# Moving the upper side of SBUF down by 224 bytes, and 128 free bytes between two pools

## The chip, the cores and the metric

The kernel runs on one core of a Trainium2 chip. The core's engines work side by side, each through its own list of instructions: TensorE (PE in the profile; its weight loads stand apart as PEld), VectorE (DVE), ScalarE (ACT), GpSimd (POOL), and SyncE (SP), which here only issues DMAs. [...] The metric is the time of one execution on the device in microseconds, the median of several runs.

A matmul has two operands in SBUF. The **stationary** one (`lhsT`, 128 by 128 here) is loaded into the array by a weight load, LDWEIGHTS in the profile. The **moving** one (`rhs`, 128 by 512) is streamed past it.

## The reference, cut to what matters

```
attention, separately in each chunk of 64 positions (8 batches, 8 heads, 576 positions, 64 wide):
    scores = q_c @ k_c^T / 8;  attn = softmax(scores);  out = attn @ v_c
x = out as (4608 tokens, 512)
h = x @ w_in                          # 512 -> 2048
g = h * clip(h + 3, 0, 6) / 6
result = g @ w_out                    # 2048 -> 512
```

All inputs and outputs are float32.

## The kernel before

**Blocks and stages.** The 4608 tokens are cut into nine blocks of 512. The first three (`NSTD = 3`) are computed in the plain way: `mm1` makes one of the 16 slices `ft` of `h`, `mm2` adds its share to the four output tiles. `SEGMENTS` gives the order: block 0 with slices 0 to 3, block 1 with slices 0 to 15, block 0 with slices 4 to 15, block 2 with slices 0 to 15. The other six blocks go in three pairs through Strassen's scheme with seven products in place of eight (`first_product`, `second_product`, lines 507 to 619). Attention of later blocks is woven between the products of earlier ones.

**Every product in three passes.** A float32 number is split into a rounded part and the rest, so `passes` (lines 220 to 224) issues three matmuls with 512 moving columns each: high by high, high by low, low by high.

```
222        PE.matmul(ps, lhsT=a_h, rhs=b_h, start=first, stop=False, skip_group_check=more)
223        PE.matmul(ps, lhsT=a_h, rhs=b_l, start=False, stop=False, skip_group_check=more)
224        PE.matmul(ps, lhsT=a_l, rhs=b_h, start=False, stop=last, skip_group_check=more)
```

In the plain stage the stationary operand is a part of a weight tile `w0` to `w15`, and the moving one is `x` (in `mm1`) or `g` (in `mm2`). Each slice of a block takes 12 matmuls in `mm1` and 12 in `mm2`, so the plain stage has 3 x 16 x 24 = 1152 of them. In the stage of the pairs the stationary operand is a part of a streamed weight tile `ws`, and the moving one is an operand tile `xop`; there are 3 x (8 x 7 x 2 x 3 + 7 x 8 x 2 x 3) = 2016 of them.

**Where tiles lie in SBUF.** Pools are stacked from two ends: most grow upwards from the bottom (the lower side), those with `side="right"` downwards from the top (the upper side). [...] The addresses that decide what follows, as the built program lists them:

| tile | role in the matmul | first byte | remainder by 64 |
|---|---|---|---|
| `w0` ... `w7` (upper side, line 57) | stationary, plain stage | 163,808 + 8192 k | 32 |
| `w8` ... `w15` (lower side, line 59) | stationary, plain stage | 39,104 + 8192 (k - 8) | 0 |
| `x` of blocks 0 to 2 (lower side) | moving, `mm1` | 22,720; 30,912; 104,640; 112,832 | 0 |
| `g` (lower side) | moving, `mm2` | 121,024 + 4096 k | 0 |
| `xop` (upper side, line 465) | moving, pairs | 163,808 + 8192 k | 32 |
| `ws` (upper side, line 466) | stationary, pairs | 139,232; 147,424; 155,616 | 32 |

The parts of a tile that a matmul reads start at multiples of 512 bytes within it. So the distance from the moving to the stationary operand has one of two remainders by 512: 0 (`w8` to `w15` with `x` or `g`, and `ws` with `xop`) or 288, which is 32 by 256 and by 64 (`w0` to `w7` with `x` or `g`).

**Change of pools.** At slot `FREE` (lines 460 to 469) the pools of the plain stage's upper side are closed: `sums` (tiles `a`, `hl`, `o`), `start` (`part`), `upper` (`w0` to `w7`). The pools `xop` (eight tiles) and `wsp` (three tiles) are opened in their place, and the first three weight tiles are fetched by SP. A tile waits for the last use of whatever lay at its bytes. From slot `SUMS` on (line 454) each engine's order is the one in which the program's lines are written; before it, a scheduler orders them.

**The start.** POOL clears `r` (line 65, called `nought` in the code), then makes `ident` (line 67). 11 matmuls on `nought` and later 56 on `ident` (line 81) keep TensorE busy while the first loads are on their way; their results are not used.

## Time and profile before

| what | value |
|---|---|
| time, median of 3 runs (lowest, highest) | 825.01 us (824.76, 825.08) |
| span of the profiled execution, first to last instruction | 822.7 us |
| mean granted TensorE clock | 1.000 |
| matmuls in the profile, all kinds | 5683 |

The profile was taken in an execution of its own, whose time the page gives as its span; 2.3 us lie between that and the median of the runs.

How to read it: a line of a group gives the source line, the engine, the operation, the tiles written and read, the shapes and the count; then the busy time in microseconds and the mean duration of one in nanoseconds, and the idle time of the engine ahead of it with what ended it. Matmuls are pipelined and their ends are modelled, so their durations overlap and say little of the pace; the pace is the distance between two starts. The view of stages gives, for each stretch, the busy time of each engine with the number of instructions that fall in it (also in part).

### The profile page before, as it was taken

To read this page: it belongs to the slowest core of one execution; us is meant where nothing else is said; L and a number is where in the kernel's file an instruction comes from. 1 tells how busy PE (TensorE), PEld (TensorE's weight loads), DVE (VectorE), ACT (ScalarE), POOL (GpSimd) and SP (SyncE) were. 2 spreads that over 40 slices of the span, in tenths; PEclk is the share of its full clock that TensorE was granted. 3 is DMA by queue.
4 is the path that set the end of the run, shared out by engine and by line. 5 is a ranking of instruction groups with operands and counts; after the bars stand their busy time and mean duration, and the time that the engine had idled before them with its cause. 6 is when DMAs were issued, how large, how long until landed. Compare 5 with 4: busy or idle time off the path is not lost.

```text
span 822.7 us, 13679 instructions
## 1 busy us (share of the span) xinstructions
PE 802.9 (98%) x5683; PEld 650.3 (79%) x5683; DVE 620.4 (75%) x753; ACT 367.1 (45%) x455; POOL 131.7 (16%) x77
## 2 busy tenths in 40 slices
PE   7889999999999999999999999999999999999998
PEld 5667888888878888788788887888788887878886
DVE  5869977877786864876989667778898567679951
ACT  4858934443444343434373432344634423336330
POOL 0000000000010000122272031222440312227100
PEclk9999999999999999999999999999999999999999
DMA  9892026677685761665646677566555664555563
GB/s 366 325 371 117 1 70 220 206 254 244 189 296 173 256 257 51 226 216 204 239 180 218 242 244 255 177 223 255 185 199 189 231 220 179 183 207 187 190 230 129
DMA packets 50158, 172.86 MB, mean 210 GB/s; under 512 B 4656, under 2 KB 17200, under 8 KB 39344
## 3 DMA queue, kind: packets, MB, share of 16 engines
q1 hardware_dynamic: 49952, 171.85, 59.3%
q8 instruction: 45, 0.74, 0.4%
q14 instruction: 17, 0.14, 0.1%
q10 hardware_dynamic: 144, 0.13, 0.0%
HBM read 133.17 MB, written 38.80 MB: 209 GB/s over the span
## 4 chain that ended last, share of the span: by engine, by line
PE 77%; DVE 13%; ACT 5%; issue 3%; DMA 1%; POOL 0%; SPq 0%; DVEq 0%; ACTq 0%
PE acc L222 17%; PE acc L224 16%; PE acc L223 16%; PE h L222 8%; PE h L224 8%; PE h L223 8%; DVE xop L381 2%; PE two L195 2%; DMA w<-w_in_out 1%; PE two L184 1%; DVE g L505 1%; DVE u L493 1%; PE two L155 1%; DVE e L165 1%; ACT r L504 1%
## 5 line engine op out<-in xcount | busy, mean ns | idle before, releaser
L222 PE MATMUL acc<-xop,ws 128*128 128x512 f32 x528 | 208.5, 396 | 4.4 <-DVE u L493 4.4
L223 PE MATMUL acc<-xop,ws 128*128 128x512 f32 x528 | 205.7, 390 | 0.0
L224 PE MATMUL acc<-xop,ws 128*128 128x512 f32 x528 | 205.3, 390 | 0.0
L222 PEld LDWEIGHTS acc<-xop,ws 128*128 128x128 f32 x528 | 99.1, 188 | 27.6 <-DVE u L493 6.8
L381 DVE TENSOR_TENSOR xop<-g,xop 128x1024 fp32r<-128x1024 f32 x72 | 103.3, 1467 | 21.5 <-ACT xop L380 21.5
L224 PEld LDWEIGHTS acc<-xop,ws 128*128 128x128 f32 x528 | 99.1, 188 | 21.1
L223 PEld LDWEIGHTS acc<-xop,ws 128*128 128x128 f32 x528 | 99.2, 188 | 19.7
L380 ACT CAST xop<-g 128x1024 fp32r<-128x1024 f32 x72 | 74.4, 1051 | 78.8 <-PE acc L224 51.3
L513 POOL TENSOR_TENSOR g<-g 128x512 f32<-128x512 f32 x24 | 34.8, 1449 | 301.2 <-DVE g L505 301.2
L222 PE MATMUL h<-x,w 128*128 128x512 f32 x192 | 76.1, 398 | 2.0 <-ACT x L204 0.9
L222 PE MATMUL acc<-g,w 128*128 128x512 f32 x192 | 76.6, 401 | 1.2 <-ACT g L236 1.2
L223 PE MATMUL h<-x,w 128*128 128x512 f32 x192 | 75.7, 394 | 0.5 <-DVE x L207 0.5
L224 PE MATMUL h<-x,w 128*128 128x512 f32 x192 | 75.5, 393 | 0.3 <-DVE w L117 0.3
L224 PE MATMUL acc<-g,w 128*128 128x512 f32 x192 | 75.4, 393 | 0.0
L223 PE MATMUL acc<-g,w 128*128 128x512 f32 x192 | 75.3, 392 | 0.0
L235 DVE SCALAR_TENSOR_TENSOR r<-r,h 128x512 f32<-128x512 f32 x48 | 32.8, 683 | 36.8 <-ACT r L234 36.7
L504 ACT ACTIVATE r<-acc,half 128x512 f32<-128x512 f32 x72 | 48.6, 687 | 26.2 <-DVE acc L493 25.3
L504 ACT ACTIVATE r<-h,half 128x512 f32<-128x512 f32 x24 | 16.5, 688 | 94.4 <-DVE h L493 94.4
L223 PE MATMUL h<-xop,ws 128*128 128x512 f32 x144 | 56.2, 390 | 0.1
L222 PE MATMUL h<-xop,ws 128*128 128x512 f32 x144 | 56.3, 391 | 0.0
L224 PE MATMUL h<-xop,ws 128*128 128x512 f32 x144 | 56.1, 389 | 0.0
L234 ACT ACTIVATE r<-h,half 128x512 f32<-128x512 f32 x48 | 33.0, 688 | 47.3 <-PE h L224 47.1
(92 smaller groups left out, 1255.3 us busy)
## 6 DMA issues: line engine op xcount, KB each, us to landing
ws<-b SPq DMA_DIRECT2D x42, 1024.0 KB, 4.9
ws<-a SPq DMA_DIRECT2D x24, 1024.0 KB, 4.9
ws<-a SPq DMA_DIRECT2D x24, 768.0 KB, 4.2
qk<-qk_in SPq DMA_DIRECT2D x17, 1024.0 KB, 6.5
w<-w_in_out SPq DMA_DIRECT2D x16, 1024.0 KB, 13.3
v<-v_in SPq DMA_DIRECT2D x17, 512.0 KB, 5.2
a<-hl SPq DMA_DIRECT2D x32, 256.0 KB, 3.3
b<-hl SPq DMA_DIRECT2D x32, 256.0 KB, 3.1
```

The costliest lines, as they stand in the source:

```text
L155: PE.matmul(self.s[o, a, c, :], lhsT=self.qk[rows, 0, c, o], rhs=self.qk[rows, 1, c, o], start=True, stop=True)
L165: DVE.tensor_tensor(out=flat(self.e), in0=flat(self.s), in1=wide(self.m), op=ALU.subtract)
L195: PE.matmul(po[o, s, a, i, :], lhsT=self.v[rows, a, i, o], rhs=self.aT[rows, a, i, o], start=True, stop=True)
L222: PE.matmul(ps, lhsT=a_h, rhs=b_h, start=first, stop=False, skip_group_check=more)
L223: PE.matmul(ps, lhsT=a_h, rhs=b_l, start=False, stop=False, skip_group_check=more)
L224: PE.matmul(ps, lhsT=a_l, rhs=b_h, start=False, stop=last, skip_group_check=more)
L234: ACT.activation(out=r, in_=h, func=AF.Relu, bias=half, scale=1.0 / 6.0)
L235: DVE.scalar_tensor_tensor(out=r, in0=r, scalar=1.0, in1=h, op0=ALU.min, op1=ALU.mult)
L380: ACT.copy(out=t[:, :, 0], in_=src)
L381: DVE.tensor_tensor(out=t[:, :, 1], in0=src, in1=t[:, :, 0].bitcast(F32), op=ALU.subtract)
L504: return (lambda: ACT.activation(out=r, in_=ps, func=AF.Relu, bias=half, scale=1.0 / 6.0), lambda: DVE.scalar_tensor_tensor(out=out, in0=r ...
L513: sub = lambda o, x, y: lambda: POOL.tensor_tensor(out=o, in0=x, in1=y, op=ALU.subtract)
```

## The change

A tile of 224 bytes is put on the upper side ahead of every other, and a tile of 128 bytes between the pools `xop` and `wsp`. Each is cleared once by POOL, and neither is read.

```diff
@@ -36,6 +36,8 @@
 WARM = 11
 WARM2 = (0, 36, 0, 6, 4)
 LAG = 2
+EDGE = 224
+GAP = 128
@@ -54,6 +56,8 @@
     std = ExitStack()
     upper = ExitStack()
+    edge = pool("edge", 1, side="right").tile([P, EDGE // 4], F32, name="edge")
+    POOL.memset(edge, 0.0)
     w_up = upper.enter_context(tc.tile_pool(name="w_up", bufs=1, side="right"))
@@ -463,6 +467,8 @@
                     upper.close()
                     xop_pool = pool("xop", 8, side="right")
+                    gap = pool("gap", 1, side="right").tile([P, GAP // 4], F32, name="gap")
+                    POOL.memset(gap, 0.0)
                     wsp = pool("wsp", 3, side="right")
                     for _ in range(3):
                         fetch()
```

So `w0` to `w7` and `xop` start at 163,584 + 8192 k (remainder 0 by 256), and `ws` at 138,880, 147,072 and 155,264 (remainder 128 by 256). Tiles of the lower side stay where they are (remainder 192 by 256). The distance from the moving to the stationary operand becomes 64 by 512 for `w0` to `w7` with `x` or `g`, 384 by 512 (128 by 256) for `ws` with `xop`, and stays 0 for `w8` to `w15`.

## The prediction

> **What bounds the kernel now.** First the page: its head, the busy times, the slices, the chain.

> ```profile
> span 822.7 us, 13679 instructions
> PE 802.9 (98%) x5683; PEld 650.3 (79%) x5683; DVE 620.4 (75%) x753; ACT 367.1 (45%) x455; POOL 131.7 (16%) x77
> PE   7889999999999999999999999999999999999998
> PEclk9999999999999999999999999999999999999999
> PE 77%; DVE 13%; ACT 5%; issue 3%; DMA 1%; POOL 0%; SPq 0%; DVEq 0%; ACTq 0%
> ```

> TensorE is busy 98% of the span at its full granted clock, and 77% of the chain that ended last is its own. What it does there is almost all matmuls of 512 columns. Such a kernel gets faster by fewer matmuls, fewer waits, or a quicker **pace**, the distance between two starts. The change touches neither the first nor, by its code, the second. So I read the pace, by the view in order of time, in three stretches without a wait: with `w1` to `w7` as stationary operands (plain stage, weights on the upper side, `x` and `g` on the lower), with `w8` to `w12` (both on the lower side), and in the pairs (`ws` and `xop`, both on the upper side). First and last start of each, then the view of stages, which counts:

> ```profile
> 73.74 0.40 PE L224 MATMUL h<-x,w 128*128 128x512 f32 x1
> ...
> 98.94 0.40 PE L224 MATMUL acc<-g,w 128*128 128x512 f32 x1
> 110.69 0.40 PE L224 MATMUL acc<-g,w 128*128 128x512 f32 x1
> ...
> 122.94 0.39 PE L224 MATMUL h<-x,w 128*128 128x512 f32 x1
> 424.73 0.39 PE L222 MATMUL acc<-xop,ws 128*128 128x512 f32 x1
> ...
> 444.91 0.39 PE L224 MATMUL h<-xop,ws 128*128 128x512 f32 x1
> ```

> ```profile
> 74.00:99.00 25.00, 25.00 (x109) 20.14 (x108) 24.62 (x31) 24.71 (x30) 0.00 (x0) 1.00 0.00 1
> 111.00:123.00 12.00, 12.00 (x55) 9.93 (x54) 8.89 (x16) 3.57 (x5) 0.00 (x0) 1.00 0.35 111
> 425.00:445.00 20.00, 20.00 (x90) 16.57 (x89) 20.00 (x11) 8.71 (x10) 11.55 (x4) 1.00 0.52 188
> ```

> The columns are the stretch, its length, and the busy time and count of PE, PEld, DVE, ACT and POOL, then clock and DMA. 109 matmuls are 108 distances: 25.20 us / 108 = 233.3 ns. The second gives 12.25 / 54 = 226.9 ns, the third 20.18 / 89 = 226.7 ns. The same instruction at the same clock takes 6.6 ns (2.9%) longer where the stationary operand lies 32 bytes off the moving one (288 by 512) than where it lies 0 off. The second stretch rules out "plain stage" as the reason, and the third, where both operands have remainder 32 by 64, rules out the remainder alone: **the distance counts**. The stretches' DMA shares (0.00, 0.35, 0.52) go the other way. This is the only thing in the trace on which a shift of addresses can act at length.

> **The change part by part.**

> *The plain stage.* Distance 32 by 256 becomes 64 by 256 for `w0` to `w7`. No row shows 64. The nearest are 32 (233.3 ns) and 0 (226.7 ns). Since both operands with remainder 0 by 64 run as quickly as both with 32, I take a repeat of 64 bytes: 64 acts as 0, and each matmul wins 6.6 ns. The other end is that 64 costs twice what 32 does: 6.6 ns lost. How many count: 3 blocks x 8 slices x 24 = 576. What precedes 66 us waits for loads and conversions; that is block 0's four slices and two `mm1` of block 1, 96 + 24 = 120. The chain also leaves TensorE for about 22 us:

> ```profile
> 215.93 0.24 PE h L224
> ...
> 234.64 1.29 issue
> 235.93 1.76 DVE g L237
> 237.68 0.61 DVE o L263
> 238.34 0.50 PE acc L222
> ```

> There the order written for DVE ends last, so what TensorE wins between 216 and 238 us (two `mm1`, 24 matmuls) only lengthens its wait. What it won ahead of 216 us is kept, since the chain comes from TensorE there. Left are 432 x 6.6 ns = 2.85 us. DVE may take some of it back: in the first stretch above it was busy 24.62 of 25.00 us and ACT 24.71, so its slack of 1.5% covers only half of the 2.9% that the 108 distances there (0.7 us) would win. I strike 0.4 us: **-2.4 us**. Ends: +2.85 us, and -6.0 us by the floor below.

> *The stage of the pairs.* Distance 0 becomes 128 by 256 for 2016 matmuls: the big lever. By a repeat of 64 bytes 128 is 0 again, and the term is **0**. No row shows 128, so both ends stay open. Worse: the 32-byte price, 2016 x 6.6 = +13.3 us. Better is bounded by the quickest pace per column in the trace, the warm-up's two-byte matmuls of 256 columns:

> ```profile
> 10.56 4.00 PE L81 MATMUL h<-ident 128*128 128x256 bf16 x35
> L81 PE MATMUL h<-ident 128*128 128x256 bf16 x56 | 6.6, 273 | 0.0
> ```

> (4.00 - 0.27) / 34 = 109.7 ns, twice that is 219.4 ns for 512 columns, 7.3 ns under the 226.7: -14.7 us for the pairs, and (233.3 - 219.4) x 432 = -6.0 us for the plain stage. The trace thus shows room below the quicker pace, but nothing that says that 128 bytes open it. I take the value of the nearest row, 0.

> [...]

> *The clearing of `edge`* goes to POOL ahead of `r`, for which the first warm-up matmul waits.

> ```profile
> L65 POOL MEMSET r<- 128x512 f32 x1 | 0.5, 525 | 0.3 <-POOLq L670 0.3
> masks.py:197 POOL MEMSET ident<- 128x128 f32 x1 | 0.2, 205 | 0.0
> L670 POOL MEMSET const-float32-0.0<- 128x1 f32 x1 | 0.1, 99 | 0.2 <-issue 0.2
> 2.80 11.63 DMA w<-w_in_out
> 14.45 1.13 ACT u L108
> ```

> Between 1 column (99 ns) and 128 (205 ns) its 56 columns take about 0.15 us. Queued behind it on POOL are `r` and `ident`; the warm-up waits for them, and is hidden by the load of `w0`, which carries the chain to 14.4 us. Cost 0; uncovered 0.15 us. Ahead of slot `SUMS` a scheduler orders the engines; one more instruction could make it pick another order. I see no reason for one, and put up to 0.5 us either way on it.

> *The clearing of `gap`* (32 columns, about 0.13 us) stands on POOL between these two:

> ```profile
> 234.43 2.71 POOL L261 TENSOR_TENSOR o<-o,part 128x512 f32<-128x512 f32 x2 [232.66 <-ACT o L260]
> 335.77 1.29 POOL L513 TENSOR_TENSOR g<-g 128x512 f32<-128x512 f32 x1 [98.63 <-DVE g L505]
> 287.55 1.84 SPq L359 DMA_DIRECT2D b<-hl  x4
> 293.82 1.28 SPq L375 DMA_DIRECT2D ws<-a  x3
> ```

> Its bytes last held `part`, read for the last time by L261 and L263 at 237 us. POOL idles for 98 us there, nobody waits for `gap`, and SP's queue is not touched. Cost 0. The 352 bytes by which `ws` sinks make its three tiles reach 128 bytes further down than the sum of their old covers: the first onto one more `o` tile (sent long before), the second onto `a`, the third onto `hl`. The stores of `hl` at 287.55 us were already waited for by the second fetch, ahead of the third on SP. So no new wait ends late, and `ws` has until 324 us.

> *Other engines.* Durations on DVE, ACT and POOL and the landing of `ws` (4.9 us, three tiles ahead) I cost at 0: TensorE's backlog hides them.

> Sum: -2.4 + 0 + 0 + 0 against the profiled 822.7 us, so a span of about 820.3; the runs' median lies 2.3 us above the span, so 825.0 - 2.4 = **822.6 us**.

> **The rivals.**

> *The pairs get quicker.* Were the reads of both operands to collide by 128 bytes and not by 64, a distance of 128 could be better than 0. For it: 226.7 ns is not the floor. Against: no row has it. With the 32-byte step again (6.6 ns) -13.3 us on the pairs and -2.4: 809.3 us; at the floor 825.0 - 14.7 - 6.0 = 804.3 us.

> *The pairs get slower.* The mechanism that costs 32 bytes 6.6 ns reaches `ws` with `xop`, as soon as its repeat is longer than 128 bytes and the best distance is 0. For it: 0 is the best distance that the trace shows. Against: both known distances fit a repeat of 64. Price 13.3 - 2.4: 835.9 us. It decides from 1.2 ns a matmul on, since 2016 x 1.2 = 2.4 us.

> *Only the plain stage gets slower.* The price grows with the distance (repeat 128): 64 costs 13.2 ns. 825.0 + 2.85 = 827.9 us.

> [...]

> **How the numbers follow.** Forecast 0.42 (its own range 821.6 to 823.6), pairs quicker 0.22, pairs slower 0.12, plain stage slower 0.10, nothing 0.14. A measurement of this kernel tells 0.2% (1.65 us) from no change. Faster: 0.22 and nearly all of the forecast's, 0.39, so 0.61; same: 0.14 and 0.03, so 0.17; slower: 0.22. A range from 803 (floor in both stages) to 829 leaves out the slower pairs and some tails, 0.18.

> **What the profile would show.** Right: in the stretch with `w1` to `w7` a pace of 226.7 ns in place of 233.3, the pairs still at 226.7, the wait at 238 us a little longer. Wrong: any other pace in the pairs, from 1.2 ns on; the plain stage at 233 or 240 ns; a PE wait for DVE between 74 and 100 us that eats the gain; another order of the instructions ahead of slot `SUMS`; a fetch of `ws` that starts well after 294 us.

## The result and the profile after

The changed kernel takes 833.38 us (median of four runs; 833.26 to 834.28) against 825.05 us before (four runs too): a ratio of 1.010, 95% interval 1.0088 to 1.0113. It is slower by 8.3 us where 2.4 us less were forecast, and it lies above the forecast range, which ended at 829 us.

The page of the changed kernel: span and busy times.

```profile
span 831.4 us, 13682 instructions
PE 813.7 (98%) x5683; PEld 651.2 (78%) x5683; DVE 620.7 (75%) x753; ACT 367.5 (44%) x455; POOL 132.0 (16%) x79
```

TensorE is busy 10.8 us longer with the same 5683 matmuls at the same granted clock (1.000 in both profiles); the other engines' busy times move by 0.4 us at most. The loss sits in the matmuls themselves. To see where, take the first and last starts of the matmuls of the pairs, by the view of the tile `ws` (minimum, median and maximum duration in ns, then first and last start in us). The kernel before comes first, then the changed one, where the same source lines have numbers higher by four:

```profile
L222 PE MATMUL acc<-xop,ws x528: 387/389/506, 324.6 to 807.3; 128*128 128x512 f32 x176
L224 PE MATMUL h<-xop,ws x144: 388/389/397, 327.8 to 818.6; 128*128 128x512 f32 x144
```

```profile
L226 PE MATMUL acc<-xop,ws x528: 390/393/504, 324.7 to 815.6; 128*128 128x512 f32 x176
L228 PE MATMUL h<-xop,ws x144: 390/393/404, 327.9 to 827.3; 128*128 128x512 f32 x144
```

The pairs begin at 324.6 and 324.7 us, so the plain stage neither won nor lost. From there to the last matmul it is 494.0 us before and 502.6 us after: the 8.6 us of the pairs are all but 0.1 us of the 8.7 by which the spans differ. The pace in the changed kernel, read as in the prediction, by first and last start and by the count in the view of stages:

```profile
73.81 0.39 PE L226 MATMUL h<-x,w 128*128 128x512 f32 x1
...
98.77 0.40 PE L228 MATMUL acc<-g,w 128*128 128x512 f32 x1
424.79 0.39 PE L228 MATMUL acc<-xop,ws 128*128 128x512 f32 x1
...
445.00 0.40 PE L228 MATMUL h<-xop,ws 128*128 128x512 f32 x1
```

```profile
74.00:99.00 25.00, 25.00 (x108) 20.12 (x107) 24.56 (x31) 24.68 (x30) 0.00 (x0) 1.00 0.00 1
425.00:445.00 20.00, 20.00 (x88) 16.20 (x87) 20.00 (x10) 8.43 (x9) 12.30 (x4) 1.00 0.48 168
```

Plain stage with `w1` to `w7`: 24.96 us / 107 = 233.3 ns, as before, though the distance from the moving to the stationary operand went from 32 to 64 bytes (by 256). Pairs: 20.21 / 87 = 232.3 ns in place of 226.7, at distance 128.

Now take every distance between two successive starts of the pairs' matmuls in the two traces. Those of up to 260 ns (about 1950 in both) sum to 442.9 us before and 454.2 us after, +11.4 us. The longer ones, at breaks for attention's matmuls and waits, sum to 51.1 and 48.4 us, -2.7 us. So a quarter of what the pace cost came back. Most of it is a wait of TensorE for DVE that got shorter:

```profile
PE acc L222 <- DVE u L493: 4.4, 6, 1.2
```

```profile
PE acc L226 <- DVE u L499: 2.6, 4, 0.7
```

Those are lines of the view of waits of the kernel before and of the changed one (us in total, times, longest): 1.8 us of the 2.7. The other 0.9 us were not traced to a wait.

The two clearings and the first fetch, by the changed kernel's view in order of time:

```profile
0.73 0.14 POOL L60 MEMSET edge<- 128x56 f32 x1 [0.29 <-POOLq L676]
238.96 0.13 POOL L471 MEMSET gap<- 128x32 f32 x1 [1.87 <-DVE o L267]
293.64 1.28 SPq L379 DMA_DIRECT2D ws<-a  x3
```

They take 0.14 and 0.13 us, `r` starts 0.08 us later than before (0.81 in place of 0.73 us), and the fetch starts no later (293.82 us before). None of it is the cause.

The new tile at the top did change the scheduler's order a little, which the forecast had named as a sign of being wrong. In the kernel before, DVE makes `g` (line 173) at 19.32 us and a `u` (line 109) two instructions later; in the changed kernel `u` comes first, at 19.42 us, and `g` at 20.02. The eight transposes on TensorE that need this `g` start at 21.39 in place of 20.70 us, and ten matmuls of attention's scores now stand ahead of them. It costs next to nothing: at 66 us TensorE stands 0.16 us ahead of the kernel before, where `gap_only`, which has the old order, stands 0.19 us behind it. `edge_only` below has the new order too.

### The profile page after: what moved, and what is told of

It reads as the page before. It is cut to its first block, busy times and chain, and to the rows that moved or that the text cites. A ratio compares the mean times of both kernels' runs of the same rounds, so it can differ in the third digit from the quotient of the medians.

```text
span 831.4 us, 13682 instructions
## 1 busy us (share of the span) xinstructions
PE 813.7 (98%) x5683; PEld 651.2 (78%) x5683; DVE 620.7 (75%) x753; ACT 367.5 (44%) x455; POOL 132.0 (16%) x79
## 2 busy tenths in 40 slices
PE   7889999999999999999999999999999999999998
## 4 chain that ended last, share of the span: by engine, by line
PE 84%; DVE 10%; ACT 4%; issue 1%; POOL 0%; DVEq 0%; ACTq 0%; POOLq 0%
PE acc L226 18%; PE acc L228 17%; PE acc L227 17%; PE h L226 9%; PE h L228 8%; PE h L227 8%; PE two L199 2%; PE two L188 1%; PE two L159 1%; DVE u L499 1%; DVE m L166 1%; DVE e L169 1%; ACT r L510 1%; DVE z L173 1%; ACT e L170 1%
## 5 line engine op out<-in xcount | busy, mean ns | idle before, releaser
L226 PE MATMUL acc<-xop,ws 128*128 128x512 f32 x528 | 211.2, 401 | 2.8 <-DVE u L499 2.6
L227 PE MATMUL acc<-xop,ws 128*128 128x512 f32 x528 | 208.4, 395 | 0.0
L228 PE MATMUL acc<-xop,ws 128*128 128x512 f32 x528 | 207.9, 395 | 0.0
L226 PE MATMUL h<-xop,ws 128*128 128x512 f32 x144 | 57.0, 396 | 0.0
L228 PE MATMUL h<-xop,ws 128*128 128x512 f32 x144 | 56.9, 395 | 0.0
L227 PE MATMUL h<-xop,ws 128*128 128x512 f32 x144 | 56.8, 394 | 0.0
```

## Experiments

One theory and its rivals to begin with. **D**: the pace is set by the distance, and all is lost in the pairs. The **rivals**: the place of the upper side itself (A), another order ahead of slot `SUMS` (O), a wait or the clearing at the new tile (W). All edits are made to the kernel before.

### The two parts alone

`edge_only` has the first part of the diff alone, `gap_only` the second:

```diff
+    edge = pool("edge", 1, side="right").tile([P, 224 // 4], F32, name="edge"); POOL.memset(edge, 0.0)
```

> The 224 bytes at the top alone; ws and xop sink together, so their distance stays 0, and w0 to w7 stand 64 bytes off x and g. Theory D (the pace is set by the distance from the moving to the stationary operand, and the loss sits in the pairs): pairs at 226.7 ns, plain stage with w1 to w7 at 233.4 ns as in the changed kernel, 825.0 us within 0.6. Rival A (the upper side's own place, remainder 0 by 256, is what costs): pairs near 232 ns and 833 us. Rival O (another order ahead of slot SUMS, or the clearing of edge): the pairs at 226.7 ns, yet 2 us or more lost ahead of 324 us.

```diff
+                    gap = pool("gap", 1, side="right").tile([P, 128 // 4], F32, name="gap"); POOL.memset(gap, 0.0)
```

> The 128 bytes between the pools alone; ws stands 128 bytes off xop, w0 to w7 stay 32 by 256 off x and g. Theory D: the whole loss is here, pairs near 232 ns, plain stage at 233.3 ns, 833.4 us within 0.8. Rival A: pairs at 226.7 ns and 825 us, since xop keeps its old place. Rival W (a late first fetch of ws): the pairs' first matmul later than 324.6 us by more than 1 us, and the pace in the pairs 226.7 ns.

The 224 bytes alone: 824.85 us, ratio 1.000 (0.9991 to 1.0009). The 128 bytes alone: 833.16 us, ratio 1.010 (1.0086 to 1.0114), and the pairs' first and last starts, by the view of `ws` of `gap_only`:

```profile
L222 PE MATMUL acc<-xop,ws x528: 390/393/504, 324.8 to 815.5; 128*128 128x512 f32 x176
L224 PE MATMUL h<-xop,ws x144: 390/393/404, 328.1 to 827.1; 128*128 128x512 f32 x144
```

That is 502.3 us for the pairs, as in the changed kernel. The gap carries the whole loss. A falls, since `xop` and `w0` to `w7` with remainder 0 by 256 cost nothing in `edge_only` (824.85 us); O falls with it, since that kernel has the clearing of `edge` and the other order too. W as a late first fetch falls as well, since the pairs begin at 324.8 us. That the new tile itself costs something is still open.

### The same tile with 256 bytes

```diff
+                    gap = pool("gap", 1, side="right").tile([P, 256 // 4], F32, name="gap"); POOL.memset(gap, 0.0)
```

> As the 128 bytes alone, with 256 bytes in their place: the same tile, clearing on POOL and covers of the old tiles, only the distance of ws from xop is a multiple of 256. Theory D with a repeat of 256 bytes: 226.7 ns in the pairs and 825.0 us within 0.6. Rival W (what costs is the tile between the pools, its clearing or the waits of the ws tiles on other old tiles): 833 us as with 128 bytes.

824.87 us, ratio 1.0002 (0.9992 to 1.0011). The same tile at the same place, cleared and waited for in the same way, costs nothing when it is 256 bytes wide; the pairs take 493.9 us, as in the kernel before (494.0). W falls altogether; the distance by 256 decides.

### Distances 0 and 256 in the plain stage

`edge_288` and `edge_32` have 288 and 32 bytes in place of the 224, and no gap.

> 288 bytes at the top and no gap: w0 to w7 stand a multiple of 512 off x and g, ws and xop stay at 0. Theory D: the plain stage with w1 to w7 at 226.7 ns, the pairs unchanged, 2.4 us gained (1.9 to 2.9), so 822.6 us, faster than both kernels. Rival A: no gain, 825 us. Rival V (what the plain stage wins is lost to DVE, which was 98% busy between 74 and 99 us): pace 226.7 ns, but new waits and under 1 us gained.

> 32 bytes at the top and no gap: w0 to w7 stand 256 by 512 off x and g. Theory D with a repeat of 256 bytes: as with 288 bytes, 226.7 ns and 822.6 us. Theory D with a repeat of 512 bytes or more: the plain stage still near 233 ns, 825.0 us within 0.5. The upper side has remainder 192 by 256 then, like the lower side; under a theory of equal remainders by 256 it is quick too.

288 bytes: 822.81 us, ratio 0.9975 (0.9965 to 0.9984). 32 bytes: 822.67 us, ratio 0.9976 (0.9967 to 0.9985). Both are faster than both kernels, by about the gain that the forecast had ascribed to 64 bytes, so rival V, with under 1 us gained, falls. `edge_288` with `w3` to `w7` as stationary operands:

```profile
86.70 0.40 PE L223 MATMUL acc<-g,w 128*128 128x512 f32 x1
...
98.95 0.39 PE L223 MATMUL acc<-g,w 128*128 128x512 f32 x1
87.00:99.00 12.00, 12.00 (x55) 9.93 (x54) 12.00 (x16) 12.00 (x15) 0.00 (x0) 1.00 0.01 1
```

12.25 us / 54 = 226.9 ns, where the kernel before had 233.3. The same columns show DVE and ACT busy for all 12.00 us: the cover is thin here, as the forecast feared. Two distances of 362 and 337 ns stand just ahead of this stretch, at 85.5 to 86.2 us. And of the 1.51 us that TensorE had won on the kernel before by 236 us, 0.24 are lost at 237 us in a wait for DVE's `o` (line 263).

Since 32 bytes do the same as 288, a distance of 256 is as good as 0. With 64 (`edge_only`, 824.85 us) and 128 (`gap_only`, 833.16 us) ruled out, the **repeat is 256 bytes**.

### A map of distances

`scan_a`, `scan_b` and `scan_c` put each `ws` tile's bytes at one of eight offsets, by turns:

```diff
-    ahead = []
+    ahead = []; shift = (0, 32, 64, 96, 128, 160, 192, 224) * 90
...
-            w = wsp.tile([P, 4, 2, 256], F32R, name="ws")
+            c = shift[len(stream)] // 4; w = wsp.tile([P, 2176], F32R, name="ws")[:, c:c + 2048].rearrange("p (n l t) -> p n l t", n=4, l=2)
```

> The kernel before, with each ws tile 512 bytes longer and its 8192 bytes put at 0, 32, 64, 96, 128, 160, 192 or 224 bytes from the tile's start, by turns from fetch to fetch, so that every distance serves some 11 of the 90 loads. Theory D with 0 as the only good distance: the matmuls at distance 0 near 227 ns, all seven others near 232 to 234 ns. Rival P (the price grows with the distance): 32 at 233, 64 at 240, and so on. Rival B (a distance better than 0 exists): one of them under 226 ns, down to 219.

> The same with 256, 288, 320, 352, 384, 416, 448 and 480 bytes. Theory D with a repeat of 256 bytes: 256 near 227 ns, the others near 233. With a repeat of 512: all eight near 233 ns. Rival B as before.

> The same with 4, 8, 12, 16, 20, 24, 28 and 512 bytes: distances within 32 bytes, and a whole repeat. Theory D by lines of 32 bytes: all but 32 itself as quick as 0, 227 ns. Theory D by lines of 16 bytes: 4 to 12 quick or in between, 16 and more near 233. 512 near 227 ns in any case. Rival B: one under 226 ns.

One run each, at a granted clock of 0.999 or 1.000: 832.53, 832.32 and 830.91 us. From the starts in the traces, the table gives the mean distance in ns between two starts, after eight matmuls at the same offset without a distance over 260 ns (95 to 157 values each):

```
offset by 256       0      4      8     12     16     20     24     28
scan_c (0: 512) 226.7  232.5  230.8  233.0  233.4  233.3  231.1  227.2

offset by 256       0     32     64     96    128    160    192    224
scan_a          226.7  233.3  233.5  234.4  232.8  233.3  228.9  233.3
scan_b (+256)   226.7  233.3  233.5  234.4  232.9  233.3  228.9  233.3
```

`scan_b` repeats `scan_a` to 0.1 ns, so the repeat of 256 is sure, and within it neither a repeat of 64 nor of 128 holds. Four bytes off are already enough (232.5 ns), so neither expectation by lines, of 32 or of 16 bytes, holds. The price doesn't grow with the distance, so rival P falls: most offsets cost 6 to 8 ns, 8 and 24 about 4, 192 costs 2.2 and 28 costs 0.5. At some offsets the price differs between the three passes: with 192, line 224 takes 226.6 ns, line 222 takes 228.6 and line 223 takes 231.2. No offset is quicker than 0, so rival B finds nothing, and 226.7 ns is the best that placing showed here.

### Which matmul pays

`low_part_off` splits each `ws` tile into the high parts and the low parts of its weights and puts the low ones 128 bytes off; `low_part_on` puts them 256 bytes off. Only the pass of line 224 has a low part as its stationary operand.

```diff
-            w = wsp.tile([P, 4, 2, 256], F32R, name="ws")
-            nc.sync.dma_start(out=w[:, :n]..., in_=t[:, :n]...)
+            w = wsp.tile([P, 2112], F32R, name="ws").rearrange("p (l m) -> p l m", l=2)[:, :, :1024].rearrange("p l (n t) -> p n l t", n=4)
+            [nc.sync.dma_start(out=w[:, :n, l].bitcast(F32), in_=t[:, :n, 256 * l:256 * l + 256]) for l in range(2)]
```

(2176 in place of 2112 in `low_part_on`.)

> The kernel before, with each ws tile in two parts, the high and the low parts of its weights, the low part 128 bytes off a multiple of 256; two DMAs a fetch. Of three passes only the one of line 224 has the low part as its stationary operand. Theory N (the load of the next matmul's weights collides with the stream of the running one): the distance from the start of line 223 to the start of line 224 grows, and with it the duration of line 223 from 389 ns to some 395, while 222 and 224 stay near 389. Theory S (a matmul's own weights count): line 224 grows. In either case about a third of the loss, 2.5 to 5 us.

> The control: the same two parts and two DMAs, with the low part at a multiple of 256. 226.7 ns on all three lines and 825 us within 0.7; what it loses against that is due to the two DMAs.

830.69 us and, for the control `low_part_on`, 824.73 us, one run each: 5.8 us lost against 824.85, where a third of the loss, 2.5 to 5 us, was expected. The groups of matmuls of `low_part_off` between 424 and 446 us (busy us, mean ns of one):

```profile
L224 PE MATMUL acc<-xop,ws 128*128 128x512 f32 x20 | 7.9, 397 | 0.0
L223 PE MATMUL acc<-xop,ws 128*128 128x512 f32 x20 | 7.9, 396 | 0.0
L222 PE MATMUL acc<-xop,ws 128*128 128x512 f32 x19 | 7.4, 389 | 0.0
```

The control has 389 on all three. In the traces of the kernel before and of the changed one a weight load of the pairs starts 3 ns (median) after the matmul ahead of its own, and in `low_part_off` the first load of line 224 and the matmul of line 223 ahead of it both start at 325.1 us. So both lines pay: 223, beside which the misplaced weights are loaded, and 224, which uses them. By the distance to the next start, over the whole stage and up to 260 ns, line 223 takes 232.4 ns, line 224 takes 233.8 and line 222 takes 227.3. Neither N alone nor S alone holds.

`moving_low_off` turns it round: the low part of the moving operand lies 128 bytes off, which line 223 alone reads.

```diff
-    small = pool("small", 4)
+    small = pool("small", 2)
...
-        return xop_pool.tile([P, 2, 2, NT], F32R, name="xop")
+        return xop_pool.tile([P, 2112], F32R, name="xop").rearrange("p (l m) -> p l m", l=2)[:, :, :1024].rearrange("p l (c n) -> p c l n", c=2)
```

> Of the three passes only that of line 223 has a moving operand (the low part of xop) 128 bytes off; all stationary operands stay at multiples of 256 from the high part. Small tiles of softmax get two buffers in place of four to make room. Theory N (the running stream against the load that runs beside it, or its own): line 223 alone is drawn out, to some 395 ns, 222 and 224 stay at 389, and a third of the loss comes back, 3 us. Theory R (a mismatch also costs the next matmul, which has to find its step again): lines 223 and 224 drawn out, 222 at 389 as with the stationary low part, 5 to 6 us. If the matmul ahead (line 222) is drawn out too, the start of the stream counts against the load ahead of it.

833.04 us, one run, against 825.08: 8.0 us, nearly the whole loss, though only one stream in three is misplaced and 3 or 5 to 6 us were expected. The pairs' distances of up to 260 ns sum to 453.7 us (454.2 in the changed kernel), so the loss is again one of pace and not of the smaller pool. Its groups between 425 and 445 us:

```profile
L224 PE MATMUL acc<-xop,ws 128*128 128x512 f32 x19 | 7.5, 395 | 0.0
L223 PE MATMUL acc<-xop,ws 128*128 128x512 f32 x19 | 7.5, 392 | 0.0
L222 PE MATMUL acc<-xop,ws 128*128 128x512 f32 x18 | 7.1, 394 | 0.0
```

All three lines are drawn out, those with operands at distance 0 no less than the other. Both theories on record, N and R, miss this; the expectation had named line 222 only as a further case. What the two runs show is that a misplaced operand also costs matmuls next to its own, against 389 ns in `low_part_on`: line 223 in `low_part_off` (396), lines 222 and 224 in `moving_low_off` (394 and 395). Why is not shown.

## Why the prediction was wrong

- **The bound, the pace, and that the distance sets it: right.** The changed kernel kept 233.3 ns in the plain stage, `gap_256` kept the old time in the pairs (493.9 us), `edge_288` turned the slower pace into the quicker (226.9 ns), and `gap_256` against `gap_only` (824.87 and 833.16 us) shows that nothing else of the gap matters.
- **The step that failed: "a repeat of 64 bytes: 64 acts as 0".** It was drawn from two known distances, 0 and 32 by 256. That both operands at remainder 0 by 64 and both at remainder 32 run alike shows that the common remainder doesn't matter; it says nothing of the repeat, since in both cases the distance is a multiple of 512. The runs put 64 at 233.3 ns (changed kernel) and 233.5 ns (map), and the repeat at 256 bytes.
- **Plain stage, -2.4 us: measured 0** (`edge_only`, ratio 1.000). The size was about right for distances 0 and 256: -2.1 and -2.2 us in `edge_288` and `edge_32`. The loss ahead of 238 us (0.24 us) and DVE's thin cover (busy 12.00 of 12.00 us) were seen in `edge_288` too.
- **Pairs, 0: measured +8.6 us.** The same assumption. The rival of the slower pairs named the price and the condition (a repeat longer than 128, 0 the best) and had 0.12. Its 835.9 us is 2.5 us high: 128 costs less than 32 in the changed kernel (232.3 in its stretch, against 233.3 ns), so +11.4 us in place of +13.3; 2.7 us came back at breaks and waits, which it left out; and the -2.4 us that it took off were not there.
- **Pairs quicker, from the floor of 219.4 ns:** no offset of the map goes below 226.7. None of the places tried reaches what lies between these two.
- **Nothing, given 0.14:** no run of the changed kernel shows the old time. It took 8.3 us more, and in the map place alone moves the pace by up to 7.7 ns a matmul (226.7 to 234.4).
- **The clearings, the covers of old tiles, SP: right at 0,** by the rows above and `edge_only` and `gap_256`. **The scheduler's order** was expected to stay and did not; the few tenths of a microsecond between runs at 66 us lie within the 0.5 us allowed for it.
- **The range** left out the slower pairs. With 32 bytes as the only priced distance but 0, that case deserved more than 0.12, and 64 and 128 should have had as much chance of the price as of none.

## What to carry to other kernels

Where matmuls run back to back, read the pace between starts separately for each pair of tiles that feeds them; a few ns between two otherwise equal groups (6.6 here) can point to where the operands lie. In this kernel it pays to keep all stationary and moving operands at one remainder by 256 bytes: 32 bytes at the top of SBUF win 2.2 us (`edge_32`), and 128 between two pools cost 8.3 (`gap_only`). Two points of an unknown function give no period: count a distance that no row shows as unknown, with the known price on it.
